# Spread sums, 14 held products, and memory V turned by DMA for the first two head blocks

## The chip, the cores and the metric

The kernel runs on one core of a Trainium2 chip. The metric is device time in microseconds: the median of several runs. One further execution was profiled; its page and trace give the durations used here.

## The reference

Two independent parts, joined along the last axis.

Part A is a linear recurrence over 2048 steps with 1024 complex states:

```
Bu = einsum('bld,pd->blp', x, B_bar)
h  = Lam_bar * h + Bu[:, t]          # for t in 0..2047
y  = 2 * einsum('blp,dp->bld', hseq, Cmat).real + x * Dskip
```

Part B is attention in 64 segments of 32 tokens with 8 memory tokens, 32 heads of 128. Each segment attends to itself (causally) and to the memory, and the output rows of the memory tokens become the next segment's memory:

```
h = concatenate([mem, xs])           # 8 + 32 rows
q, k, v = h @ Wq, h @ Wk, h @ Wv
o = softmax(mask(q k^T * scale)) v;  o = o @ Wo
mem = o[:, :8];  outs.append(o[:, 8:])
```

## The kernel before

The program has four stages, and TensorE has work in all of them.

**Stage 1** (to about 347 us) mixes the first half of part A with the value projection of part B. A list made by `steps()` sets the order: 32 blocks `("s", pc, q)` of part A (8 groups of 128 states, times 4 stretches of 512 time steps; block number n = 4*pc + q) and 32 steps `("v", hb, q)` of the value projection (8 blocks of 4 heads, times 4 stretches of 512 tokens). Most blocks are followed by one value step; after blocks 6, 11, 16, 21, 26 and 30 there is none. `stage1` does 16 matmuls into `psU` (two buffers of two banks). VectorE then multiplies by a table into `a_pr` (L273), adds (L278), and scans (L283, two of them); ScalarE copies the scans to `a_g` (L284); GpSimd works out the carry (L288 to L290). The product with the second table, `a_n` (L297), and its sum, `a_h` (L298), belong to `form()`, which is called inside the next block, between that block's multiply and its add; SP stores `a_h` to `a_hs`. `tables(pc + 1)` is made in block 4*pc + 2. A value step does 32 matmuls into `psP` (three banks), ScalarE copies each bank to a staging buffer `b_vst` (L93; two of these buffers, taken in turn by `next_st`), and ScalarE's queue stores the buffer to `b_vx` in DRAM (L498 to L502).

Between these lies `sum_x`: 16 reductions of `b_xe` (the turned input) to sums over segments (L433), one for each 128 tokens, and a last step that makes `xbar` (L439 to L443). It is a generator, and block n takes two steps of it after `stage1`. `xbar` feeds a guess of the memory rows: `og` multiplies it with the value weights, `guess` with the output weights, and the guess is put into columns of `b_xe` called `memT`.

**Stage 2** (about 347 to 470 us) is the second half of part A: 32 units of 16 matmuls and a VectorE add (`a_ot`, L339); each second unit ScalarE's queue stores `a_ot`. Beside it run the remaining `og`, `guess`, and at the end the memory rows of V for the first two head blocks: `v_mem(0)` and `v_mem(1)`. `v_mem` multiplies weights with `memT`, which gives the rows turned (channels by rows), copies them to `b_vm`, turns them, and stores them to `b_vx` and `b_vt`. For head blocks 2 to 7 (called from stage 3) the turn is a write to DRAM (`b_vmt`) and a DMA transpose into a staging buffer; for 0 and 1 it is four TensorE transposes.

**Stage 3** (about 470 to 1017 us) mixes the q and k projections of a head pair (`proj`) with attention over groups of 96 tokens (`attention`); `load_v` brings values of a head pair from `b_vx` and `b_vt` on SP's queue. **Stage 4** is the output projection. A branch at the end repeats the work step by step should the guess have been too coarse; it isn't taken here.

Instructions are put in order by a planner that works with estimated times and can move an instruction past others of its engine. `keep_in_program_order` holds one at its place in the program. Everything on TensorE is held in stage 1, everything on SP in stages 1 and 2, and on VectorE the 16 reductions, all 32 products L297 and one constant of the check. In stage 3 nothing is held but a few loads. Pools named `p1`, `p2` and so on share memory, and a tile waits until the tile that lay there is done with.

Of the kernel before, what the change touches and what calls it, by code (L numbers as in the profile page):

```python
# [9 lines left out]
BF16 = mybir.dt.bfloat16  # L10
# [24 lines left out]
NMX = 7  # L35
# [9 lines left out]
EO = E + 4  # L45
MW = 4 * GP + 24

XMAIN = 1920
XE = T + NM
XP = 2128  # L50
# [108 lines left out]
class PartA:  # L159
# [101 lines left out]
    def stage1(self, pc, tb):  # L261

        k = self.k; V, S, G, PE = k.V, k.S, k.G, k.PE
        if tb == 0:
            self.carry = None
        self.form, last = None, self.form
        t3, r3 = self.tabs
        u = k.ps("U", (128, 2, TB))
        for i in range(2):
            for c in range(KC):  # L270
                PE.matmul(u[:, i, :], self.bt[:, i, c, :], self.xT[:, c, tb * TB:(tb + 1) * TB], start=(c == 0), stop=(c == KC - 1))
        pr = self.wp.tile([128, 2, 2, TB], FP32, name="a_pr", bufs=2)
        V.tensor_tensor(pr[:], u[:].unsqueeze(1).to_broadcast([128, 2, 2, TB]),  # L273
                        view(t3, [[TB + 1, 2], [TB + 1, 2], [1, TB]]), ALU.mult)
        if last is not None:
            last()
        w = pr[:, :, 0, :]
        V.tensor_tensor(w, w, pr[:, :, 1, :], ALU.add)  # L278
        rb = self.rr[:, pc:pc + 1].to_broadcast([128, TB])
        ini = self.carry  # L280
        g = self.wp.tile([128, 2, TB], BF16, name="a_g", bufs=2)
        for j in range(2):
            V.tensor_tensor_scan(w[:, j, :], rb, w[:, j, :], 0.0 if ini is None else ini[:, j:j + 1], ALU.mult, ALU.add)  # L283
            S.activation(g[:, j, :], w[:, j, :], ACT.Copy)  # L284
        if tb < NB - 1:
            nx = self.wp.tile([128, 2], FP32, name="a_nx", bufs=2); tt = self.wp.tile([128, 2], FP32, name="a_tt", bufs=2)
            for j in range(2):
                G.tensor_scalar(tt[:, j:j + 1], w[:, j, TB - 1:TB], t3[:, 1, TB:TB + 1], None, ALU.mult)  # L288
                G.tensor_scalar(nx[:, j:j + 1], w[:, 1 - j, TB - 1:TB], t3[:, 2 - 2 * j, TB:TB + 1], None, ALU.mult)
            G.tensor_tensor(nx[:], nx[:], tt[:], ALU.add)  # L290
            self.carry = nx

        def form():
            n = self.wp.tile([128, 2, 2, TB], BF16, name="a_n", bufs=1)
            h = self.wp.tile([128, 2, TB], BF16, name="a_h", bufs=2)
            k.tc.keep_in_program_order(
                V.tensor_tensor(n[:], g[:].unsqueeze(1).to_broadcast([128, 2, 2, TB]), view(r3, [[TB, 2], [TB, 2], [1, TB]]), ALU.mult))  # L297
            V.tensor_tensor(h[:], n[:, :, 0, :], n[:, :, 1, :], ALU.add)  # L298
            k.SP.dma_start(self.hs[tb][:, pc, :, :], h[:])
        self.form = form  # L300
# [48 lines left out]
class PartB:  # L349
# [195 lines left out]
        yield  # L545


    def store_t(self, hb, s):

        for r0, n, i in ((0, 2, NMX), (NTL - 3, 2, NMX + 2), (3, NTL - 6, NT4)):  # L550
            self.k.SP.dma_start(self.vt[hb][r0:r0 + n, :].rearrange("n (h e) -> n h e", h=4), s[i:i + n, :, :])

    def v_mem(self, hb, w=None):
        k = self.k
        w = w or self.load_wv(hb)
        p = k.ps("P")
        for h in range(4):
            for c in range(KC):
                k.PE.matmul(p[:, h * NM:(h + 1) * NM], w[:, c, h * 128:(h + 1) * 128], self.memT[:, c, :], start=(c == 0), stop=(c == KC - 1))
        vm = self.vmp.tile([128, 4, 128], BF16, name="b_vm", bufs=1)  # L560
        k.copy("v", vm[:, :, 0:NM], p[:, 0:4 * NM].rearrange("p (h n) -> p h n", h=4))
        if hb > 1:

            k.V.memset(vm[:, :, NM:128], 0.0)
            k.SP.dma_start(self.vmt[hb][:], vm[:].rearrange("p h n -> p (h n)"))
            yield
            s = self.next_st()[:].rearrange("p i h e -> p (i h e)")[:, 0:576].rearrange("p (h e) -> p h e", h=4)
            k.V.memset(s[:, :, E:EW], 1.0)
            k.SP.dma_start_transpose(s[:, :, 0:E], self.vmt[hb][:])
            yield  # L570
            k.SP.dma_start(self.vx[hb][64:64 + NMX, :].rearrange("n (h e) -> n h e", h=4), s[0:NMX, :, 0:EW])
            self.store_t(hb, s[:, :, 0:EW])
            yield
        yield
        pt = k.ps("P", (128, 1024), BF16)
        for h in range(4):
            k.PE.transpose(pt[0:NM, h * 128:(h + 1) * 128], vm[:, h, 0:NM], k.ident[:])
        st = self.next_st()
        k.copy("v", st[0:NM, 0, :, 0:E], pt[0:NM, 0:512].rearrange("p (h e) -> p h e", h=4))
        sv = st[:, 0, :, :].rearrange("p h e -> p (h e)")  # L580
        k.SP.dma_start(self.vx[hb][64:64 + NMX, :], sv[0:NMX, :])
        self.store_t(hb, st[:, 0, :, :])
        yield


# [425 lines left out]
def kernel_main(tc, A_x, A_Lre, A_Lim, A_Bre, A_Bim, A_Cre, A_Cim, A_logdt, A_Dskip, B_x, B_mem0, B_Wq, B_Wk, B_Wv, B_Wo, out,  # L1011
                force=False, dbg=None):
    with ExitStack() as ctx:
# [16 lines left out]
        with pool("p1x", "right") as p1x, pool("p1", "right", 1) as p1:  # L1030
            a.tab = a.tmp = a.wp = a.btp = p1
            k.pin |= {"PE", "SP"}
            warm(k, p1)
            w0 = b.wl.tile([128, KC, 512], BF16, name="b_wv", bufs=2)
            b.load_wv_part(w0, 0, 0, 128, nc.scalar)
            b.x0 = []
            for i in range(2):
                b.load_x0(p1, i)
            b.load_wv_part(w0, 0, 128, 256)
            b.load_wv_part(w0, 0, 256, 512)  # L1040
            b.load_xp(64 + 256, 256, 256)
            wv = {0: w0, 1: b.load_wv(1)}
            consts(k)
            a.load_params(p1)
            b.load_m0(p1)
            b.stage_init()
            order = steps()
            b.v_x(0, 0, wv[0])
            b.load_x(1)
            a.load_b(0)  # L1050
            a.xT = p1x.tile([128, KC, T], BF16, name="a_xT", bufs=1)
            a.load_x(0)
            a.params(p1, p1)
            b.init(p1)
            a.tables(0)
            loads = [[(b, 2)], [(a, 1), (a, 2)], [(b, 3), (a, 3)]]
            sx = b.sum_x(p1)
            tabs = {0: a.tabs}
            bts = {0: a.bt}
            for kind, pc, q in order[1:]:  # L1060
                if loads and kind == "v":
                    for o, n in loads.pop(0):
                        o.load_x(n)
                if kind == "v":
                    b.v_x(pc, q, wv[pc])
                    if q == 3:
                        if pc >= 3:
                            b.og(pc, wv[pc])
                        n = (pc + 2) if pc + 2 < PC else (2, 0)[pc + 2 - PC]
                        wv[n] = b.load_wv(n)  # L1070
                    continue
                a.tabs, a.bt = tabs[pc], bts[pc]
                n = 4 * pc + q
                if q == 2 and pc + 1 < PC:
                    a.load_b(pc + 1)
                    bts[pc + 1], a.bt = a.bt, bts[pc]
                if pc >= 4 and q == 1:
                    a.load_c(pc - 4)
                a.stage1(pc, q)
                for _ in range(2):  # L1080
                    next(sx, None)
                if q == 2 and pc + 1 < PC:
                    a.tables(pc + 1)
                    tabs[pc + 1] = a.tabs
                if n == 12:
                    masks(k)
                    check_consts(k)
                if n == 14:
                    b.fill(p1)
            a.form()  # L1090
            k.pin.remove("PE")
# [7 lines left out]
        with pool("p2h", "right") as p2h, pool("p2", "right") as p2:  # L1099
# [5 lines left out]
            for i, _ in enumerate(s2):  # L1105
                if i in (1, 4, 7):
                    n = (2, 0, 1)[(i - 1) // 3]
                    b.og(n, wv[n], "O")
                    if n == 2:
                        wv[1] = b.load_wv(1)  # L1110
                if i in (3, 7, 11, 15):
                    b.load_wog((3, 7, 11, 15).index(i), p2)
                if i in (9, 11, 13, 15, 17, 19, 21, 22):
                    next(g)
                if i == 20:
                    b.load_wqk(0)
                if i == 23:
                    for _ in g:
                        pass
                if i in (24, 26):  # L1120
                    vm = b.v_mem((i - 24) // 2, wv[(i - 24) // 2])
                if 24 <= i < 28:
                    next(vm)


# [131 lines left out]
```

## Time and profile before

| | us |
|---|---|
| median of 7 runs | 1241.37 (1241.06 to 1241.55) |
| profiled execution | 1241.22 |
| its span, first to last instruction | 1239.5 |
| TensorE busy with matmuls | 1231.1 |
| VectorE, ScalarE, GpSimd busy | 676.2, 266.7, 268.7 |
| granted TensorE clock | 1.00 |

The 1.72 us between the span and the profiled time lie around the span. A row of the timeline gives the start in us, the time in us from the first start to the last end of the instructions merged in it, the engine, the line, the operation, output and input by the program's names, and how many; in brackets at its end stand the idle time of the engine just ahead of it and what ended that. "ACTq" and "SPq" are the engines' DMA issues. In the table of stretches each engine has its busy time in us and its number of instructions, and then come the TensorE clock, the DMA share and GB/s.

### The profile page before, as it was taken

What the parts mean: (1) busy time and instruction counts of PE and PEld (TensorE: products, weight loads), DVE (VectorE), ACT (ScalarE), POOL (GpSimd) and SP (SyncE); (2) the same over time, 40 slices, a digit from 0 to 9 for tenths busy, and PEclk for the clock granted to TensorE, in tenths of its full rate; (3) what the DMA queues carried; (4) which work ended last, traced back from release to release, by engine and by line L of the source; (5) the groups of instructions that cost most, each with busy time, mean ns of one, the idle gap of its engine ahead of it and who ended that gap; (6) DMA issues with size and microseconds to landing.
All of it is one profiled execution on the core that took longest, in us unless ns stands there. A gap on an engine that the chain in (4) does not pass through costs nothing.

```text
span 1239.5 us, 20045 instructions
## 1 busy us (share of the span) xinstructions
PE 1231.1 (99%) x8174; PEld 654.8 (53%) x8174; DVE 676.2 (55%) x1270; ACT 266.7 (22%) x694; POOL 268.7 (22%) x437
## 2 busy tenths in 40 slices
PE   9999999999999999999999999999999999999998
PEld 4444444444445555656565656555565554445444
DVE  4799999988721124666666666656666641001000
ACT  5344444443310000112121111212111210000000
POOL 4111221212222321222222222223222320000000
PEclk9999999999999999999999999999999999999999
DMA  9942455563798834765464645536474279407000
GB/s 242 249 148 79 139 139 131 158 157 98 212 319 257 268 111 103 211 145 129 108 153 108 153 108 117 137 89 138 113 148 103 58 208 248 102 18 154 18 17 27
DMA packets 321268, 174.20 MB, mean 141 GB/s; under 512 B 145882, under 2 KB 308876, under 8 KB 321172
## 3 DMA queue, kind: packets, MB, share of 16 engines
q1 hardware_dynamic: 299076, 145.33, 48.8%
q10 hardware_dynamic: 21072, 24.38, 5.9%
q0 software_dynamic: 1024, 3.17, 0.7%
q8 instruction: 65, 1.06, 0.4%
q14 instruction: 31, 0.25, 0.1%
HBM read 84.42 MB, written 53.96 MB: 112 GB/s over the span
## 4 chain that ended last, share of the span: by engine, by line
PE 92%; DVE 4%; DMA 2%; issue 1%; SPq 1%; ACT 0%; ACTq 0%; DVEq 0%
PE psP L68 78%; PE psU L68 7%; PE psS L68 3%; PE psO L68 2%; PE psR L68 1%; DMA b_vx<-b_vst 1%; DVE a_pr L283 1%; DVE a_pr L273 1%; DVE b_xr L433 1%; SPq L68 1%; DVE a_pr L278 1%; DMA b_wv<-in_B_Wv_dram 0%; ACT b_vst L93 0%; DVE a_h L298 0%; DVE a_tabh L239 0%
## 5 line engine op out<-in xcount | busy, mean ns | idle before, releaser
L68 PE MATMUL psP<-b_xe,b_wk 128*128 128x480 bf16 (+1 forms) x1280 | 247.5, 343 | 0.0
L68 PE MATMUL psP<-b_xe,b_wq 128*128 128x480 bf16 (+1 forms) x1280 | 247.5, 343 | 0.0
L68 PE MATMUL psP<-b_wv,b_xe 128*128 128x512 bf16 (+2 forms) x1048 | 224.8, 373 | 2.5 <-ACT b_vst L93 2.1
L685 POOL TENSOR_TENSOR b_m<-b_e,maskB 99x396 bf16<-99x396 bf16 (+1 forms) x160 | 134.4, 840 | 335.9 <-ACT b_e L684 335.9
L684 ACT ACTIVATE b_e<-psS 99x396 bf16<-99x396 f32 (+3 forms) x208 | 91.3, 441 | 530.7 <-PE psS L68 522.3
L68 PEld LDWEIGHTS <-b_wk 128*128 128x128 bf16 x1280 | 119.2, 98 | 94.2
L68 PEld LDWEIGHTS <-b_xe 128*128 128x128 bf16 x1056 | 101.8, 98 | 122.1 <-issue 3.4
L68 PEld LDWEIGHTS <-b_wq 128*128 128x128 bf16 x1280 | 118.5, 98 | 87.8
L95 DVE CAST b_k<-psP 128x480 bf16<-128x480 f32 (+1 forms) x192 | 97.3, 528 | 100.4 <-PE psP L68 100.4
L95 DVE CAST b_q<-psP 128x480 bf16<-128x480 f32 (+1 forms) x192 | 97.3, 528 | 92.2 <-PE psP L68 90.9
L68 PEld LDWEIGHTS <-b_ol 128*128 128x128 bf16 x864 | 84.3, 98 | 94.4
L68 PE MATMUL psU<-a_xT,a_bt 128*128 128x512 bf16 x512 | 114.8, 379 | 0.0
L68 PE MATMUL psP<-t,a_hl 128*128 128x512 bf16 x512 | 113.1, 379 | 0.0
L95 DVE CAST b_ost<-psP 128x512 bf16<-128x512 f32 (+1 forms) x17 | 11.5, 676 | 177.6 <-PE psP L68 177.6
L93 ACT ACTIVATE b_vst<-psP 128x512 bf16<-128x512 f32 x126 | 72.8, 590 | 108.5 <-PE psP L68 101.2
L68 PE MATMUL psP<-wo,b_ol 128*128 128x512 bf16 (+1 forms) x448 | 92.5, 364 | 0.0
L68 PE MATMUL psP<-t,b_ol 128*128 128x512 bf16 x416 | 92.2, 379 | 0.0
L288 POOL TENSOR_SCALAR a_tt<-a_pr,a_tabf 128x1 f32<-128x1 f32 x48 | 36.6, 762 | 251.3 <-DVE a_pr L283 251.3
L702 DVE TENSOR_TENSOR b_ob<-psO,b_accR 99x384 bf16<-99x384 f32 x160 | 86.0, 554 | 2.6 <-DVE b_accR L701 0.4
L273 DVE TENSOR_TENSOR a_pr<-psU,a_tabf 128x2048 f32<-128x2048 f32 x32 | 73.0, 2282 | 26.4 <-PE psU L68 26.4
L68 PEld LDWEIGHTS <-a_bt 128*128 128x128 bf16 x512 | 49.8, 98 | 59.5
L68 PEld LDWEIGHTS <-a_hl 128*128 128x128 bf16 x512 | 49.1, 98 | 56.7
(203 smaller groups left out, 963.5 us busy)
## 6 DMA issues: line engine op xcount, KB each, us to landing
b_v<-b_vx SPq DMA_DIRECT2D x16, 1122.0 KB
b_wv<-in_B_Wv_dram SPq DMA_DIRECT2D x16, 1024.0 KB
b_vx<-b_vst ACTq DMA_DIRECT2D x24, 544.0 KB
b_on<-b_ob SPq DMA_DIRECT2D x15, 720.0 KB
a_hs<-a_h SPq DMA_DIRECT2D x32, 256.0 KB
b_wog<-in_B_Wo_dram SPq DMA_DIRECT2D x4, 2048.0 KB
b_wq<-in_B_Wq_dram SPq DMA_DIRECT2D x16, 512.0 KB
b_wk<-in_B_Wk_dram SPq DMA_DIRECT2D x16, 512.0 KB
```

The lines of the kernel that those rows point to most:

```text
L68: r = f(*a, **kw)
L93: self.S.activation(out, in_, ACT.Copy)
L95: self.V.tensor_copy(out, in_)
L273: V.tensor_tensor(pr[:], u[:].unsqueeze(1).to_broadcast([128, 2, 2, TB]), view(t3, [[TB + 1, 2], [TB + 1, 2], [1, TB]]), ALU.mult)
L278: V.tensor_tensor(w, w, pr[:, :, 1, :], ALU.add)
L283: V.tensor_tensor_scan(w[:, j, :], rb, w[:, j, :], 0.0 if ini is None else ini[:, j:j + 1], ALU.mult, ALU.add)
L288: G.tensor_scalar(tt[:, j:j + 1], w[:, j, TB - 1:TB], t3[:, 1, TB:TB + 1], None, ALU.mult)
L433: r = V.tensor_reduce(xs[:, :, 4 * j:4 * j + 4], self.xe[:, :, 128 * j:128 * j + 128].rearrange("p c (s t) -> p c s t", s=4), AX.X, ALU.add)
L684: k.S.activation(e[:, a:b, :, 0:n], s[0:GW, a:b, :, 0:n], ACT.Exp, scale=float(E) ** -0.5, accum_out=self.accE[0:GW, j:j + 1])
L685: k.G.tensor_tensor(mv[:, a:b, :, 0:n], e[:, a:b, :, 0:n], mask[0:GW, :, 0:n].unsqueeze(2).to_broadcast([GW, b - a, 2, n]), ALU.mult)
L702: V.tensor_tensor(self.ob[:, b0:b0 + n, :], o[0:GW, 0:n, 0:E], r.unsqueeze(2).to_broadcast([GW, n, E]), ALU.mult)
```

## The change

1. Block 0 takes two steps of `sum_x` ahead of `stage1` and three after it; blocks 1 to 9 take 2, 2, 2, 0, 2, 1, 1, 1, 1. It was two after each block until the 17 steps were through.
2. The product L297 is held in program order for the first 14 blocks (`HELD`) alone.
3. `v_mem` turns by DMA for every head block. For the first two, all its DMAs (the write, the transpose and the four stores) are issued on ScalarE's queue; the calls take three units of stage 2 each, from units 24 and 27, in place of two from 24 and 26.

```diff
+HELD = 14
...
+        held = NB * pc + tb < HELD
+
         def form():
...
-            k.tc.keep_in_program_order(
-                V.tensor_tensor(n[:], g[:].unsqueeze(1).to_broadcast([128, 2, 2, TB]), view(r3, [[TB, 2], [TB, 2], [1, TB]]), ALU.mult))
+            i = V.tensor_tensor(n[:], g[:].unsqueeze(1).to_broadcast([128, 2, 2, TB]), view(r3, [[TB, 2], [TB, 2], [1, TB]]), ALU.mult)
+            if held:
+                k.tc.keep_in_program_order(i)
...
-    def store_t(self, hb, s):
+    def store_t(self, hb, s, q):
...
-            self.k.SP.dma_start(self.vt[hb][r0:r0 + n, :].rearrange("n (h e) -> n h e", h=4), s[i:i + n, :, :])
+            q.dma_start(self.vt[hb][r0:r0 + n, :].rearrange("n (h e) -> n h e", h=4), s[i:i + n, :, :])
...
         k.copy("v", vm[:, :, 0:NM], p[:, 0:4 * NM].rearrange("p (h n) -> p h n", h=4))
-        if hb > 1:
...
+        q = k.SP if hb > 1 else k.nc.scalar
+        k.V.memset(vm[:, :, NM:128], 0.0)
+        q.dma_start(self.vmt[hb][:], vm[:].rearrange("p h n -> p (h n)"))
         yield
-        pt = k.ps("P", (128, 1024), BF16)
-        for h in range(4):
-            k.PE.transpose(pt[0:NM, h * 128:(h + 1) * 128], vm[:, h, 0:NM], k.ident[:])
-        st = self.next_st()
-        k.copy("v", st[0:NM, 0, :, 0:E], pt[0:NM, 0:512].rearrange("p (h e) -> p h e", h=4))
...
+        s = self.next_st()[:].rearrange("p i h e -> p (i h e)")[:, 0:576].rearrange("p (h e) -> p h e", h=4)
+        k.V.memset(s[:, :, E:EW], 1.0)
+        q.dma_start_transpose(s[:, :, 0:E], self.vmt[hb][:])
+        yield
+        q.dma_start(self.vx[hb][64:64 + NMX, :].rearrange("n (h e) -> n h e", h=4), s[0:NMX, :, 0:EW])
+        self.store_t(hb, s[:, :, 0:EW], q)
         yield
...
+                for _ in range(2 if n == 0 else 0):
+                    next(sx)
                 a.stage1(pc, q)
-                for _ in range(2):
-                    next(sx, None)
+                for _ in range((3, 2, 2, 2, 0, 2, 1, 1, 1, 1)[n] if n < 10 else 0):
+                    next(sx)
...
-                if i in (24, 26):
-                    vm = b.v_mem((i - 24) // 2, wv[(i - 24) // 2])
-                if 24 <= i < 28:
+                if i in (24, 27):
+                    vm = b.v_mem((i - 24) // 3, wv[(i - 24) // 3])
+                if 24 <= i < 30:
                     next(vm)
```

More of the change, by code (lines that the diff above doesn't have):

```diff
@@ L561, in v_mem @@
         k.copy("v", vm[:, :, 0:NM], p[:, 0:4 * NM].rearrange("p (h n) -> p h n", h=4))
-        if hb > 1:
[L564 to L573, printed above, removed]
-        yield
-        pt = k.ps("P", (128, 1024), BF16)
-        for h in range(4):
-            k.PE.transpose(pt[0:NM, h * 128:(h + 1) * 128], vm[:, h, 0:NM], k.ident[:])
-        st = self.next_st()
-        k.copy("v", st[0:NM, 0, :, 0:E], pt[0:NM, 0:512].rearrange("p (h e) -> p h e", h=4))
-        sv = st[:, 0, :, :].rearrange("p h e -> p (h e)")
-        k.SP.dma_start(self.vx[hb][64:64 + NMX, :], sv[0:NMX, :])
-        self.store_t(hb, st[:, 0, :, :])
+        q = k.SP if hb > 1 else k.nc.scalar
+        k.V.memset(vm[:, :, NM:128], 0.0)
+        q.dma_start(self.vmt[hb][:], vm[:].rearrange("p h n -> p (h n)"))
+        yield
+        s = self.next_st()[:].rearrange("p i h e -> p (i h e)")[:, 0:576].rearrange("p (h e) -> p h e", h=4)
[4 more added lines that the diff above has]
+        self.store_t(hb, s[:, :, 0:EW], q)
         yield
```

## The prediction

> **What bounds the kernel now.** I read the page first: TensorE carries the span, and the chain that ended last is almost all TensorE.
>
> ```profile
> PE 1231.1 (99%) x8174; PEld 654.8 (53%) x8174; DVE 676.2 (55%) x1270; ACT 266.7 (22%) x694; POOL 268.7 (22%) x437
> PE 92%; DVE 4%; DMA 2%; issue 1%; SPq 1%; ACT 0%; ACTq 0%; DVEq 0%
> ```
>
> Busy time alone does not say that TensorE runs at its peak, so I took the spacing of matmul starts from the trace. A 512-column matmul follows the one before by 0.216 us nearly everywhere. After the start-up, 10 us in, gaps worth more than 0.1 us above that spacing are few: 1.10 us at 120.1, 0.43 at 131.6, 0.81 at 336.0, 0.45 at 343.7, and about 0.1 at 1152.6. The first four sum to 2.79 us. **This is all that better ordering can give back**; everything else on TensorE is work.
>
> The second view is the busy time by stretch (columns: PE, PEld, DVE, ACT, POOL, clock, DMA):
>
> ```profile
> 40.00:60.00 20.00, 20.00 (x94) 9.11 (x93) 17.51 (x15) 7.48 (x13) 4.09 (x10) 1.00 1.11 252
> 100.00:120.00 20.00, 20.00 (x94) 9.11 (x93) 20.00 (x17) 7.48 (x14) 4.03 (x10) 1.00 0.36 111
> 120.00:140.00 20.00, 18.80 (x88) 8.32 (x86) 19.95 (x23) 8.38 (x16) 5.32 (x7) 1.00 0.41 121
> 180.00:200.00 20.00, 20.00 (x94) 9.08 (x93) 14.79 (x13) 8.52 (x15) 2.07 (x5) 1.00 0.43 127
> 320.00:340.00 20.00, 19.35 (x90) 8.71 (x89) 14.95 (x12) 6.80 (x12) 6.47 (x13) 1.00 0.52 181
> ```
>
> VectorE has 2.5 us free at 40 to 60, nothing from 100 to about 180, then slack again. TensorE loses matmuls (88 and 90 for 94) where VectorE is full, and at the end of the stage.
>
> The third view, the timeline, shows how the loss happens:
>
> ```profile
> 117.77 2.45 DVE L283 TENSOR_TENSOR_SCAN a_pr<-a_rr,a_nx,a_pr 128x512 f32<-128x512 f32 x2
> 120.25 0.63 ACT L284 ACTIVATE a_g<-a_pr 128x512 bf16<-128x512 f32 x1
> 120.79 0.58 ACT L93 ACTIVATE b_vst<-psP 128x512 bf16<-128x512 f32 x1
> 121.42 1.89 PE L68 MATMUL psP<-b_wv,b_xe 128*128 128x512 bf16 x8 [0.94 <-ACT b_vst L93]
> ...
> 337.04 7.07 PE L68 MATMUL psP<-b_wv,b_xe 128*128 128x512 bf16 x32 [0.65 <-ACT b_vst L93]
> ...
> 343.75 1.57 ACT L93 ACTIVATE b_vst<-psP 128x512 bf16<-128x512 f32 x3 [4.19 <-DMA b_vx<-b_vst]
> 344.40 1.89 PE L68 MATMUL psP<-b_wv,b_xe 128*128 128x512 bf16 x8 [0.29 <-ACT b_vst L93]
> ```
>
> The scan of block 7 ends late on VectorE; ScalarE stands in front of its copy of that scan (`a_g`); the copies out of `psP` queue behind it; the three `psP` banks are full; TensorE stops. At 343.75 the cause is another: ScalarE waits for a staging buffer whose store, issued at 331.87, lands 11.8 us later.
>
> [...] the trace agrees (a 512-column matmul has 0.379 us of duration but 0.216 us of spacing), so I count spacing. [...]
>
> **The change, part by part.** Blocks are numbered n = 4*pc + q, 0 to 31.
>
> *Sums earlier.* Still 17 steps. Finished after blocks 0 to 9: 5, 7, 9, 11, 11, 13, 14, 15, 16, 17; before: 2, 4, 6, 8, 10, 12, 14, 16, 17, 17. One sum is 1.16 us of VectorE (two take 2.32). Two now stand before block 0, when VectorE is free (6.4 us idle before 33.70), and their columns of `b_xe` are turned by TensorE before 10 us. The third extra one falls into the 2 us gap between the sums at 45.21 and the multiply of block 1 near 49.7. So 3 x 1.16 = 3.5 us moves into idle time. It is taken out after block 4 (two) and block 6 (one). A VectorE block with two sums takes 9.68 us (multiplies at 112.70 and 122.38), so 8.5 with one.
>
> Working it forward: the multiply of block 5, today at 93.35, comes at 91.0, when its matmuls are done. That of block 6, today 103.03, would be at 100.7, but its matmuls end near 101.4: 0.7 us idle. Block 7: 101.4 + 8.5 = 109.9 for today's 112.70, so the scan ends 7.5 later, at 117.4 for 120.2, and ScalarE's copy frees the bank at about 118.6. TensorE wants it at 120.3. **Gap of 1.10 gone, cover 1.7 us.** Block 8: multiply 118.4, scan ends 125.9, with the table step and the copies the bank is free near 128.3; TensorE, 1.1 us earlier than today, wants it at 130.7. **Gap of 0.43 gone, cover 2.4 us.** After that VectorE is about 2.8 us earlier and TensorE 1.53, so no new gap. `xbar`, today at 130, comes a block later; its first reader is the `og` product at 168.46. The sums cost nothing else. Sum: -1.53.
>
> *Products held in 14 blocks.* No instruction goes or comes; 18 products (1.22 us each, with a 0.69 add behind) may move. There is slack on VectorE there, and TensorE loses nothing between 132 and 336. The likely new place is the wait for matmuls, such as the 2.83 us before 320.89, ahead of the next multiply. At the end this brings the scan of block 31 about 1.9 us forward, enough for the 0.81 gap; but the next one hangs on the store that lands at 343.66, and TensorE would only arrive there earlier and wait longer. The product of block 31 (347.59, today behind the `og` copy) can start near 336.5, but its store stays behind a weight load on SP's queue, at 349.56. Bounds for the part: nothing, or -1.26 if the store is early as well; a loss is possible where a product gets ahead of a multiply that is ready (1.9 us, against about 2.7 us of cover at a bank, 255.73 to 258.4). I take -0.2.
>
> *Memory V turned by DMA.* Removed: eight TensorE transposes, 0.055 us apart, 0.22 us for each head block (448.15 to 448.37 and 456.32 to 456.54), with no wait around them: **-0.44**. Also removed: two VectorE copies of 0.41 and eight SP issues; added: four memsets (0.25 and 0.09) on VectorE, which has 2.5 us idle per unit of 3.45; and on ScalarE's queue per head block one write, one transpose and four stores. That chain is seen on SP for head block 2: write issued 567.23, transpose 569.22, last store issued by 577.7, so 10.5 us. On ScalarE's queue it starts near 445.7 and 456.9 (the second matmuls now start a unit later, at 455.0) and ends near 456 and 468. Behind it wait only three output stores with two buffers; the first Exp is at 486.42, a cover of 18 us. `load_v(0)` needs the first chain, landed near 458; today its long load is issued at 460.70, takes SP 16.2 us, and is first used at 491.43. SP is freed of the second set of stores, the weight load for `v_mem(3)` moves 3 us. Cost 0 under those covers; without them it is what the chain overruns.
>
> **Sum:** 1.53 + 0.2 + 0.44 = 2.17 us off the profiled execution (1241.22: span 1239.5 and 1.72 around it): 1239.05. The median of the runs is 0.15 higher, so **1239.2**. A change under 0.2% (2.48 us) can't be told from none by this measurement.
>
> **Rivals.**
>
> 1. *All gaps go* (0.15): 2.79 + 0.44 = 3.23 off, 1238.1. For it: the 0.81 gap is a VectorE lateness that the freed products should cure. Against: the DMA at 343.66.
>
> 2. *The sums only move the lateness*, or the planner does not place them early: VectorE is full until 180 and the totals by block 7 are alike. Then only the transposes and the tail count: -0.5, 1240.9. Against: 3.5 us of real idle time before.
>
> 3. *Slower: VectorE waits for the new DMA chain.* The planner pulls the memsets of head blocks 2 and 3 (L568 at 452.73 and 460.98) directly behind the stores that free their staging buffer. Now these stores end the 10.5 us chain, about 458 and 470. If VectorE stands at such a memset while `psP` fills, TensorE stops. In stage 2 there is cover of two units (6.9 us), in the first projections of two groups of 1.62 us. A memset that waits 6 us in the projections costs 6 - 3.2 = 2.8, twice that with the `b_vm` memset; net +0.6 to +3.4, 1242 to 1244.8. It decides from a wait of 3.2 us there plus the 2.2 gained. For it: VectorE already waited for DMA semaphores before 452.73. Against: the order is planned with DMA times in mind.
>
> 4. *The transpose on ScalarE's queue isn't what runs*: then the ident matmuls remain and 0.44 is missing; unlikely (0.03), it is written out.
>
> **How the numbers follow.** Main case 0.55, 1238.6 to 1239.8; its better quarter (0.13) passes the bound. All gaps 0.15, rival 2 with 4 0.10, slower 0.20 (with planner moves in the attention that I can't see). So faster 0.13 + 0.15 = 0.28, same 0.42 + 0.10 = 0.52, slower 0.20. Range: from 1237.6 (all gaps and run scatter) to 1244.0, which takes in most of rival 3.
>
> **What would show it.** Right: 94 matmuls in each 20 us from 100 to 200; no PE wait near 120; five sums before 50 us; no `psP<-ident,b_vm` group; transposes of `b_vst` on ACTq for two head blocks; first att_back matmul about 2 us earlier. Wrong: a PE wait ended by a DVE instruction between 450 and 490; new PE gaps between 180 and 330; a first Exp later than 486.

## The result, and the profile after

| | before | after |
|---|---|---|
| median, us | 1241.38 (34 runs) | 1244.65 (14 runs, 1244.24 to 1246.4) |
| ratio, with its 95% interval | | 1.0028 [1.0021, 1.0035] |
| profiled execution, and its span | 1241.22, 1239.5 | 1245.2, 1243.4 |

The change makes the kernel **slower by 3.3 us**. The forecast was 1239.2 with a range up to 1244.0, so the kernel moved the other way, to just outside the range.

The page still shows a TensorE that is busy for 99% of the span, with eight matmuls fewer (the transposes). In the chain that ended last VectorE's share has gone from 4% to 0, and the DMA's from 2% to 3%:

```profile
PE 1232.0 (99%) x8166; PEld 654.5 (53%) x8166; DVE 679.9 (55%) x1272; ACT 266.4 (21%) x694; POOL 271.6 (22%) x437
PE 96%; DMA 3%; SPq 1%; ACTq 0%; DVE 0%; issue 0%; DVEq 0%
```

In the table of stretches (PE, PEld, DVE, ACT, POOL, clock, DMA share, GB/s) stage 1 has its matmuls back: 95, 94 and 95, where 94, 88 and 90 stood. The loss is at the end of stage 2, with 2.98 us of PE missing from 440 to 460, and 2.20 from 460 to 480 at a granted clock of 0.91. The first row is the kernel before, where nothing was missing there:

```profile
440.00:460.00 20.00, 20.00 (x155) 10.48 (x154) 5.31 (x11) 0.00 (x0) 6.90 (x5) 1.00 0.53 167
```

```profile
100.00:120.00 20.00, 20.00 (x95) 9.01 (x94) 19.41 (x16) 8.04 (x15) 2.12 (x5) 1.00 0.27 91
120.00:140.00 20.00, 20.00 (x94) 9.08 (x93) 19.96 (x23) 7.77 (x15) 4.56 (x10) 1.00 0.47 134
320.00:340.00 20.00, 20.00 (x95) 9.00 (x94) 14.78 (x12) 6.74 (x12) 7.09 (x14) 1.00 0.60 214
440.00:460.00 20.00, 17.02 (x134) 8.71 (x132) 3.04 (x7) 0.00 (x0) 2.78 (x2) 1.00 0.43 136
460.00:480.00 20.00, 17.80 (x95) 9.28 (x95) 6.21 (x26) 0.00 (x0) 4.14 (x6) 0.91 0.22 69
```

By the spacing of matmul starts, all four gaps of stage 1 are gone (2.79 us). New, counted above the usual spacing, are a stop of 3.48 us at 456.64, eight matmuls after it at up to 0.427 us instead of 0.216 (1.5 us more), and a stop of 2.02 us at 473.51, where the matmuls have 199 columns and a spacing of 0.086: **7.0 us**. So 7.0 - 2.79 - 0.44 = 3.8 us longer; the span grew by 3.9 and the median by 3.3.

The timeline of the queues, VectorE and TensorE points to the cause. The first row merges two loads of weights, issued at 442.20 and 453.60. The rows of ACTq are head block 0's *chain*: the write, the transpose, which needs the write's data, and the four stores, which need the transpose's. A DMA *lands* when its data have arrived.

```profile
442.20 11.78 SPq L69 DMA_DIRECT2D b_wv<-in_B_Wv_dram  x2
...
442.70 0.34 ACTq L568 DMA_DIRECT2D b_vmt<-b_vm  x1
448.06 1.32 ACTq L572 DMA_TRANSPOSE b_vst<-b_vmt  x1
...
450.79 1.41 ACTq L574 DMA_DIRECT2D b_vx<-b_vst  x1
...
452.24 2.33 ACTq L555 DMA_DIRECT2D b_vt<-b_vst  x3
...
459.60 0.09 DVE L571 MEMSET b_vst<- 128x32 bf16 x1 [9.73 <-DMA b_vt<-b_vst]
459.60 0.68 DVE L343 TENSOR_TENSOR a_ot<-psP,a_xd 128x512 bf16<-128x512 f32 x1
...
460.34 12.05 PE L69 MATMUL psP<-t,a_hl 128*128 128x512 bf16 x48 [3.31 <-DVE a_ot L343]
...
474.78 0.09 DVE L571 MEMSET b_vst<- 128x32 bf16 x1 [8.52 <-DMA b_vt<-b_vst]
...
475.62 1.53 PE L69 MATMUL psP<-b_xe,b_wk 128*128 128x199 bf16 x16 [1.86 <-DVE a_ot L343]
```

The 0.09 us memset of ones at 459.60 prepares a staging buffer for head block 2. In the kernel before the same memset waited for nothing:

```profile
452.73 0.09 DVE L568 MEMSET b_vst<- 128x32 bf16 x1
```

Here it stands in VectorE's queue ahead of the add that empties `psP`, and it waits 9.73 us until the last store of head block 0's chain has left that buffer, 16.7 us after the chain's write was issued (442.70; the store landed at 459.44). Meanwhile `psP` fills and TensorE stops. It happens again at 474.78, for head block 3 behind head block 1.

The view of waits (total, times, longest), here from 440 to 480, puts both kinds of memset side by side; the second kind is the zeros of `b_vm`:

```profile
DVE b_vst L571 <- DMA b_vt<-b_vst: 18.3, 2, 9.7
...
DVE b_vm L567 <- DMA b_vmt<-b_vm: 9.8, 2, 5.5
...
PE psP L69 <- DVE a_ot L343: 5.2, 2, 3.3
```

### The profile page after: what moved, and what is told of

It reads as the page before. It is cut to its first block, busy times and chain, and to the rows that moved or that the text cites. A ratio compares the mean times of both kernels' runs of the same rounds, so it can differ in the third digit from the quotient of the medians.

```text
span 1243.4 us, 20035 instructions
## 1 busy us (share of the span) xinstructions
PE 1232.0 (99%) x8166; PEld 654.5 (53%) x8166; DVE 679.9 (55%) x1272; ACT 266.4 (21%) x694; POOL 271.6 (22%) x437
## 3 DMA queue, kind: packets, MB, share of 16 engines
q0 software_dynamic: 1024, 3.17, 0.7%
## 4 chain that ended last, share of the span: by engine, by line
PE 96%; DMA 3%; SPq 1%; ACTq 0%; DVE 0%; issue 0%; DVEq 0%
PE psP L69 80%; PE psU L69 9%; PE psS L69 3%; PE psO L69 2%; PE psR L69 1%; DMA b_vt<-b_vst 1%; DMA b_vmt<-b_vm 1%; SPq L69 1%; DMA b_wv<-in_B_Wv_dram 0%; DMA b_vst<-b_vmt 0%; ACTq L555 0%; ACTq L574 0%; DVE a_ot L343 0%; DVE b_vm L96 0%; DVE b_ost L96 0%
```

## Experiments

I asked three questions: does each part bring what it was priced at; does the memset make the stop; and why is the chain 16.7 us long? Each kernel's edit is against the changed kernel, except for the four under "The parts alone", which apply one or two parts to the kernel before. All times are medians, with the ratio to the kernel before on the same chip.

### The parts alone

**Sums earlier, alone**

```diff
+                for _ in range(2 if n == 0 else 0):
+                    next(sx)
                 a.stage1(pc, q)
-                for _ in range(2):
-                    next(sx, None)
+                for _ in range((3, 2, 2, 2, 0, 2, 1, 1, 1, 1)[n] if n < 10 else 0):
+                    next(sx)
```

> The kernel before with the early sums alone. The prediction's step: both TensorE gaps near 120 and 131 us (1.10 and 0.43) go, so 1.5 us less than before, about 1239.8. If the products also had to be let loose for that, one of the two gaps stays and the gain is 1.1 or less. The gaps at 336 and 344 (0.81 and 0.45) should stay.

Measured: 1239.74, ratio 0.9988 [0.9981, 0.9994], which is -1.56 us with an interval of -2.4 to -0.7, so a change below the 2.48 us that the prediction took for the limit does show here. Both gaps near 120 and 131 are gone. At the end of the stage the gap of 0.81 stays, and the other grows from 0.45 to 0.94: TensorE gets there earlier and waits longer for the same store. By its gaps this kernel gains 1.53 - 0.49 = 1.04, inside the interval.

**14 products held, alone**

```diff
+        held = NB * pc + tb < HELD
...
+            if held:
+                k.tc.keep_in_program_order(i)
```

> The kernel before with the products held in the first 14 blocks only. The gaps near 120 and 131 stay. If the late scan of block 31 is all that causes the end of the stage to stall, the gap of 0.81 goes, and the one of 0.45 behind the store grows by as much (net 0, as the prediction had it); if the store comes early as well, both go: 1.26 us less, about 1240.1.

Measured: 1240.04, ratio 0.9989 [0.9983, 0.9996], -1.26 us. Both gaps at the end of stage 1 are gone, the other two stay, and a small one of about 0.18 us appears at 201.7, in the stretch where the prediction wanted to see no new ones (the changed kernel has none there). The timeline shows the product moved, as the prediction had it, into the wait for the matmuls. But the wait for the store, expected to stay, has more than halved (4.19 us at 343.75 before):

```profile
317.48 1.23 DVE L296 TENSOR_TENSOR a_n<-a_g,a_tabh 128x2048 bf16<-128x2048 bf16 x1 [0.70 <-ACT a_g L284]
...
321.03 2.29 DVE L273 TENSOR_TENSOR a_pr<-psU,a_tabf 128x2048 f32<-128x2048 f32 x1 [1.59 <-PE psU L68]
...
340.82 0.60 ACT L93 ACTIVATE b_vst<-psP 128x512 bf16<-128x512 f32 x1 [1.94 <-DMA b_vx<-b_vst]
```

The store was issued later than before (334.60 for 331.87) and landed earlier (340.8 for 343.7). Before, it was issued between GpSimd's four `a_hl` loads (330.02 to 332.24); here it comes 3.6 us after them. The trace's DMA records fit this: before, the store's 512 packets ran for 6.5 us with 429 packets of GpSimd's loads among them; here they run for 2.3 us with 80 among them. No run moved the store alone.

**The DMA turn, alone**

```diff
-        if hb > 1:
+        q = k.SP if hb > 1 else k.nc.scalar
...
+        k.V.memset(s[:, :, E:EW], 1.0)
+        q.dma_start_transpose(s[:, :, 0:E], self.vmt[hb][:])
...
-                if i in (24, 26):
+                if i in (24, 27):
```

> The kernel before with the DMA turn of memory V on ScalarE's queue alone. If the loss of the changed kernel sits wholly in the waits of VectorE's memsets on that chain: 0.44 us less for the transposes and 6.9 us more for the gaps seen near 457, 461 and 474, so about 6.4 us more than before, 1247.8. If the loss needs the new order of stage 1 (TensorE arriving earlier), clearly less than that, 4 us or under.

Measured: 1247.15, ratio 1.0048 [1.0034, 1.0062], +5.85 us. The stop (3.5 us at 459.2), slow matmuls after it (the next three units took 12.21 us, where 0.216 us a matmul makes 10.5) and a second stop (1.5 at 476.3) are all there. The loss belongs to this part alone.

**Sums and 14 held, without the DMA turn**

> The kernel before with the early sums and the products held in 14 blocks, memory V turned on TensorE as before. If the two parts work on different gaps, their gains (1.56 and 1.26) add: 2.8 less than before, about 1238.5, and no gap above 0.1 us between 100 and 480 us. If they share VectorE's slack, one of them is worth less: 1239 or more.

Measured: 1238.45, ratio 0.9977 [0.9967, 0.9986], -2.95 us, as much as the two alone (1.56 + 1.26 = 2.82) and as the four gaps (2.79). The parts add up.

### Is it the memset?

**Fills made once.** The fills are the two kinds of memset. The zeros go into two fixed `b_vm` buffers at the start of the program; the ones are written only in the first round of the two staging buffers.

```diff
+        self.vms = [c.tile([128, 4, 128], BF16, name=f"b_vm{i}") for i in range(2)]
...
+        for vm in self.vms:
+            k.G.memset(vm[:, :, NM:128], 0.0)
...
-        vm = self.vmp.tile([128, 4, 128], BF16, name="b_vm", bufs=1)
+        vm = self.vms[hb % 2]
-        k.V.memset(vm[:, :, NM:128], 0.0)
...
-        k.V.memset(s[:, :, E:EW], 1.0)
+        if hb < 2:
+            k.V.memset(s[:, :, E:EW], 1.0)
```

> The changed kernel, but the zeros of b_vm are written once, at the start, into two fixed buffers, and the ones of the staging buffers only for head blocks 0 and 1 (the later head blocks find them in place). So no memset in stages 2 and 3 has to wait for the DMA chain; the chain itself is unchanged. Memset theory: the gaps of 6.9 us go, 3.2 us less than before, about 1238.2. If the chain's length on ScalarE's queue (late V, late output stores) or the planner's order in the attention is what costs, the time stays above 1241.

Measured: 1242.53, ratio 1.0007 [1.0001, 1.0014], 4.3 us above the expectation. The stops at 457 and 474 are gone, so the memset theory holds for them. But **a second wall**, another wait that stops TensorE, stood behind the first: TensorE now waits in the attention for the values of V. The first row below is the load of V in the kernel before, the others are this kernel's (the row of a load merges a small first part and the main one).

```profile
460.43 16.49 SPq L68 DMA_DIRECT2D b_v<-b_vx  x2
```

```profile
464.20 16.99 SPq L69 DMA_DIRECT2D b_v<-b_vx  x2
...
491.23 0.50 PE L69 MATMUL psO<-b_v,b_m 128*128 128x129 bf16 x6 [2.96 <-DMA b_v<-b_vx]
```

The main load of V came 9 us later than before (issued at 469.62 instead of 460.70), and landed at 491.19. In the changed kernel it came later still (472.91, landed 494.15) and cost nothing, because TensorE, some 7 us later by its stops, asked for it only at 495.32. The one loss hid the other. The profiled execution, at 1240.87, is among this kernel's shortest; its runs reach from 1240.3 to 1243.8, which the last section takes up.

**Only the ones written once**, and **only the zeros written once**, split that edit.

> The changed kernel with only the ones of the staging buffers written once; the zeros of b_vm are still written each time. If the memsets of the staging buffers make the two gaps (waits of 9.7 and 8.5 us, beyond the cover), the gaps near 457 and 474 go and the wait for V of e4_once is left: 1240.5 to 1243. If the b_vm memsets (waits of 5.5 and 4.2) are enough for a gap: 1244 or more.

> The other half: the zeros of b_vm once, the ones of the staging buffers each time. If the staging memsets make the gaps: 1243 to 1245, with gaps of some 2 us or more near 457 and 474. If both kinds are needed for a gap: as e4_once, 1240.5 to 1243.

Measured: ones once, 1242.89, 1.0009 [1.0000, 1.0017]; zeros once, 1244.96, 1.0036 [1.0022, 1.0049]. With the ones written once, VectorE still waits up to 7.8 us at a memset of zeros and TensorE doesn't stop near 457; with the zeros written once, it stops as before. These are the waits of VectorE, first in the kernel with the ones once, then in the one with the zeros once:

```profile
DVE b_vm L567 <- DMA b_vmt<-b_vm: 13.3, 2, 7.8
```

```profile
DVE b_vst L573 <- DMA b_vt<-b_vst: 17.0, 2, 9.8
```

**The memset of ones makes the stop.** A wait of 7.8 us at the zeros was covered, one of 9.8 at the ones was not.

### Why is the chain so long?

**The chain on SP's queue**

```diff
-        q = k.SP if hb > 1 else k.nc.scalar
+        q = k.SP
```

> The changed kernel with the DMA chain of the first two head blocks on SP's queue in place of ScalarE's. Theory that VectorE's memsets wait for the chain, whatever queue it is on: the gaps near 457 and 474 stay, 1243 to 1247. Theory that ScalarE's queue is what is slow: the chain takes about 10.5 us as for head block 2, the gaps go, 1239.5 or less.

Measured: 1246.0, ratio 1.0040 [1.0026, 1.0054]. This fits neither expectation. The first hop, from the issue of the write to that of the transpose, is just as long (442.55 to 448.08), so leaving ScalarE's queue doesn't shorten it; but here the write comes behind a load of weights on its own queue. The stops at 457 and 474 are gone: the second load of weights is now issued at 454.18, behind the chain's stores, the last of them lands at 456.89 instead of 459.44, and the memsets of ones wait only 3.1 and 4.5 us. Yet the time is no better. The load of V now stands behind both chains on SP (main load 468.18, landed 494.24), and the wait at it, with slow matmuls after it (480 columns at 0.400 us for 0.202), is the loss.

```profile
PE psO L69 <- DMA b_v<-b_vx: 5.9, 1, 5.9
```

**Weight loads held back.** In the changed kernel SP issues the two loads of value weights for head blocks 2 and 3 (1 MB each) at 442.20 and 453.60. The first goes out 0.5 us ahead of the write of head block 0's chain, the second 0.1 us ahead of that chain's last store (453.67, landed 459.44). Here they come in stage 3 and are held there; nothing else in the program differs.

```diff
+    def load_wv_late(self, hb):
+        w = self.wl.tile([128, KC, 512], BF16, name="b_wv", bufs=2)
+        self.k.tc.keep_in_program_order(self.k.SP.dma_start(w[:], self.Wf[2][:, :, hb * 512:hb * 512 + 512]))
+        return w
...
+            if hp == 0 and u in (5, 8):
+                late[2 + u // 8] = b.load_wv_late(2 + u // 8)
...
-                    vm = b.v_mem(hp // 2 + 1)
+                    vm = b.v_mem(hp // 2 + 1, late.pop(hp // 2 + 1, None))
```

> The changed kernel, but the two 1 MB weight loads for head blocks 2 and 3, which SP issues at 442.2 and 453.6 as the chain starts, are held back to stage 3. Theory that the chain's hops are long (5.4 us for the write, 5.8 for the last store) because these loads share the DMA engines: hops of 2 to 3 us, VectorE waits about 4 us less at each memset, the gaps of 6.9 us fall to 1.5 or less: 1238 to 1240. Theory that the hops are long by themselves: no change, 1244.6.

Measured: **1237.79**, ratio 0.9972 [0.9961, 0.9983], -3.6 us: faster than both kernels. The memsets are still there and still wait, but only 2.75 us for the first and 5.98 for the second, and TensorE has no wait left from 440 to 520:

```profile
442.41 0.34 ACTq L573 DMA_DIRECT2D b_vmt<-b_vm  x1
444.14 1.32 ACTq L577 DMA_TRANSPOSE b_vst<-b_vmt  x1
...
448.16 2.33 ACTq L560 DMA_DIRECT2D b_vt<-b_vst  x3
...
452.33 0.09 DVE L576 MEMSET b_vst<- 128x32 bf16 x1 [2.75 <-DMA b_vt<-b_vst]
...
459.78 16.93 SPq L69 DMA_DIRECT2D b_v<-b_vx  x2
...
466.91 0.09 DVE L576 MEMSET b_vst<- 128x32 bf16 x1 [5.98 <-DMA b_vt<-b_vst]
```

The first hop takes 1.7 us (442.41 to 444.14) instead of 5.4, the last store 2.5 to its landing instead of 5.8, and the chain 9.7 (to 452.1) instead of 16.7. From 440 to 450 the DMA engines were busy for 0.18 of the time here, and 0.42 in the changed kernel (next to the last column); these are the two rows, this kernel's first:

```profile
440.00:450.00 10.00, 10.00 (x75) 5.12 (x74) 2.78 (x5) 0.00 (x0) 2.50 (x2) 1.00 0.18 55
```

```profile
440.00:450.00 10.00, 10.00 (x76) 5.04 (x74) 2.63 (x5) 0.00 (x0) 1.53 (x2) 1.00 0.42 131
```

The trace's DMA records show the write's packets behind the load's. Issued at 442.70, its 128 packets start from 446.25 on, when 766 of the load's 1024, the first of them at 443.23, have started; without the load they start at 443.26. The store of stage 1 above had 429 packets of GpSimd's loads among its own; here most of the load has started before the write's first packet. Why, no run tested. What the runs show is that the hop of this write, issued 0.5 us behind a 1 MB load of another queue, is longer by 3.7 us than without that load. The main load of V moved up as well, to 464.98; it landed at 486.62 and was used at 488.02. **With the weight loads held back neither wall stands.** Early, they lengthen the chains (head block 0's to 16.7 us from 9.7), for which VectorE's memsets wait and behind which the load of V comes. The DMA turn is then worth about its price: 1237.79 with it and 1238.45 without it, 0.66 us for the 0.44 forecast, with intervals that overlap.

**Both edits together** (fills once, weight loads held back):

> Both cures: the fills written once (as in e4_once) and the weight loads held back (as in e7_late). In e4_once TensorE then waited 3 us at 488 us for V. If that wait comes from the same long hops (the load of V is behind the chain of head block 1), it goes: 3.2 us less than before, 1238.1 with little scatter. If V is late for another reason, 1240 to 1243 as in e4_once.

Measured: 1237.74, ratio 0.9971 [0.9959, 0.9982]. Nothing is gained over the late weight loads alone: here the memsets, whose wait is covered, cost nothing (1237.79 with them).

### What holds the load of V?

In the changed kernel's waits of SP's queue, from 440 to 512, two lines belong to the two loads of head pair 0:

```profile
SPq L69 <- DMA b_vst<-b_vmt: 7.6, 1, 7.6
...
SPq L69 <- DMA b_vx<-b_vst: 5.2, 1, 5.2
```

These loads read head block 0, but here they wait for the transpose and a store of head block **1**. By the changed kernel's trace it is no dependence of data. The transpose and the first load carry one semaphore, number 118: the transpose landed at 467.47, and the load, which waits for 118, went out at 467.49. The store and the main load carry number 100: landed 472.89, issued 472.91. To test whether head block 1's chain holds the load, that chain was moved into stage 3, on SP's queue (with the fills once, and the weight loads early as in the changed kernel).

```diff
-        q = k.SP if hb > 1 else k.nc.scalar
+        q = k.SP if hb > 0 else k.nc.scalar
+        if hb == 1:
+            yield
...
-                if 24 <= i < 30:
+                if 24 <= i < 28:
...
+            if hp == 0 and u in (4, 6, 8):
+                next(vm)
```

> As e4_once (fills written once, weight loads early), but the DMA chain of head block 1 is issued in stage 3 on SP's queue, behind the first loads of V. In e4_once the two loads of V (reading head block 0) went out at the moment at which transfers of head block 1's chain landed. Theory that V is late only because its loads stand behind that chain: they go out near 460 or before, no wait of TensorE at 488, 1238 to 1238.8. If the load of V is late through the weight loads themselves, the wait stays: 1240 to 1243.

Measured: 1246.47, ratio 1.0039 [1.0025, 1.0053]; missed. The run didn't do what its edit meant: the planner took the chain back ahead of the load (454.17 to 467.8), whose main part was issued at 468.66 and landed at 494.29. TensorE waited for it, and the granted clock of the profiled execution was 0.997 on average, where the kernel before has 1.00.

```profile
PE psO L69 <- DMA b_v<-b_vx: 5.8, 1, 5.8
```

The same, with the six DMAs of that chain held in program order:

```diff
+        def kp(i):
+            if hb == 1:
+                k.tc.keep_in_program_order(i)
```

> e9_once_chain1 again, with the transfers of head block 1's chain held in program order on SP, so that they really come behind the first loads of V (in e9_once_chain1 the planner moved them ahead, and the loads of V went out at 468.3). The weight loads stay early. Theory that V is late because its loads stand behind the chain of head block 1: they go out near 460, V lands before 488, no wait of TensorE there: 1237.7 to 1238.8. If V is late through the weight loads alone, the wait at 488 stays, 1240 to 1243.

Measured: 1237.72, ratio 0.9971 [0.9960, 0.9983], where the fills once alone gave 1242.53. SP's timeline has the load ahead of the chain again, and no wait of TensorE is left, though the weight loads are as early as in the changed kernel:

```profile
441.95 11.78 SPq L69 DMA_DIRECT2D b_wv<-in_B_Wv_dram  x2
...
460.82 0.27 SPq L69 DMA_DIRECT2D b_v<-b_vt  x1
461.14 16.72 SPq L69 DMA_DIRECT2D b_v<-b_vx  x2
```

So, with the weight loads early, the second wall is the place of the V load behind head block 1's chain. That the shared semaphore alone holds it, in the kernels with the chain on ScalarE's queue, is read from the trace; no run changed the semaphores by themselves.

## Why the prediction failed

**What bounds the kernel: right.** The four gaps were worth 2.79 us, and all four went.

**Sums earlier, -1.53: right, with one omission.** Alone, the part gave 0.49 of its gaps back at the store of stage 1, which "so no new gap" had left out. The worked path shows in the changed kernel's timeline, with the multiplies of blocks 6, 7 and 8 at 101.61, 110.17 and 118.72, where 101.4, 109.9 and 118.4 were forecast, and the scan of block 7 over at 117.7 (117.4):

```profile
101.61 2.29 DVE L274 TENSOR_TENSOR a_pr<-psU,a_tabf 128x2048 f32<-128x2048 f32 x1 [0.59 <-PE psU L69]
...
110.17 2.28 DVE L274 TENSOR_TENSOR a_pr<-psU,a_tabf 128x2048 f32<-128x2048 f32 x1
...
115.24 2.46 DVE L284 TENSOR_TENSOR_SCAN a_pr<-a_rr,a_nx,a_pr 128x512 f32<-128x512 f32 x2
```

**14 held, -0.2: the term was too small**, and measured -1.26, the far bound. The failing step was "the next one hangs on the store that lands at 343.66": the landing was taken as fixed. It moved by 2.9 us when the issues around it moved.

**DMA turn, -0.44 and "Cost 0 under those covers": here the sign went wrong.** The transposes went, as priced. The cost was 7.0 us in place of 0, by three steps of the working. The third made the stops; the first made them longer; the second hid the next one.

1. The chain's length, 10.5 us, came from head block 2's row, and it ends with the issue of the last store, which landed at 579.31: 12.1 us after the write's issue, for 16.7 here. That row is no quiet moment (from 565 to 580 the DMA engines were busy for 0.71 of the time, with a 1 MB load at 571.72), but no 1 MB load of another queue was issued just ahead of its steps. The write's hop took 2.0 us there and 5.4 here. Of the loads of weights in this stretch the prediction says only that one "moves 3 us".

```profile
567.23 0.54 SPq L68 DMA_DIRECT2D b_vmt<-b_vm  x1
569.22 1.91 SPq L68 DMA_TRANSPOSE b_vst<-b_vmt  x1
571.72 0.38 SPq L68 DMA_DIRECT2D b_wv<-in_B_Wv_dram  x1
```

2. The cover of the V load was counted from today's issue (460.70) to today's first use (491.43). The load landed at 486.75, some 10 us after SP had done issuing it, so the real cover was 4.7 us. The change moved the load by 12.
3. The working asked who waits behind ScalarE's queue and found only covered work, and it priced the memsets by their 0.25 and 0.09 us. The one that waited was VectorE, for a buffer that the chain reads: its memset of ones waited 9.73 us. The length of the chain is not the whole of it. The chain started 3 us sooner than forecast and landed at 459.44, where the forecast had "near 458"; had it landed at 458, TensorE would still have stopped for about 2 us, an estimate from the 3.48 us less the 1.44.

**The rival "VectorE waits for the new DMA chain" is what happened**, given 0.20. It named the instruction, the head blocks and both memsets; its top price, 1244.8, is close to 1244.65. Its mechanism is right, but that nearness is partly luck. The first stop comes in stage 2, where the rival counted two units of cover (6.9 us): the wait of 9.73 ran over. And its price had no half-rate matmuls. The words against it, "the order is planned with DMA times in mind", were no evidence: the planned order had the wait of 9.73 us in it. The sign that was to show the forecast wrong, a TensorE wait ended by VectorE between 450 and 490, is in the profile twice.

**What stays open.** The gaps account for 3.23 us of the 3.6 that the late weight loads gain over the kernel before; the other 0.4 was not placed. Why the store of stage 1 lands earlier is read from the trace and not tested. Why the write's packets start so late behind a load of the other queue isn't known.

## What to carry to other kernels

A price for a chain of small dependent DMAs must come from a moment with the same neighbours: ask which large loads the new order puts just ahead of its steps, on any queue (here the write's hop took 5.4 us behind a load of SP's, and 1.7 without it). When a DMA is put in place of compute, list which instructions wait for its buffers and what stands behind them, above all fills ahead of an instruction that empties PSUM (here the memset of ones, 9.73 us), and which later loads come behind it. A cover ends where the data land, not where the issue ends (486.75, not 476.9, for the load of V in the kernel before); and when one wall falls, look for the next wait before counting the gain.

## What the runs showed of the hardware

**A stop can cost more than its own length.** After the stop of 3.48 us, TensorE ran at half rate for 2.9 us (0.427 us a matmul for 0.216), and after the 6.1 us of the chain on SP's queue at 0.400 for 0.202 (480 columns; three of them took 1.41 us, and 0.77 with the fills once). After 2.02 us it ran at full rate (0.085 us a matmul of 199 columns, for 0.086 ahead of the stop). With the DMA turn alone, the three units after the stop of 3.53 us took 12.21 us, 1.7 more than 0.216 a matmul makes. Stops of 3.1 us go both ways: no slow matmul followed with the fills once (the wait of 2.96 us shown above), and nearly 6 us of half rate with the ones once (a wait of 2.94). This is the latter's row of stretches, with a clock of 0.66, and its first eight 480-column matmuls after the stop, which took 1.78 us in the other:

```profile
490.00:500.00 10.00, 8.89 (x45) 4.70 (x45) 3.60 (x9) 0.63 (x3) 0.87 (x1) 0.66 0.17 46
```

```profile
491.71 3.41 PE L69 MATMUL psP<-b_xe,b_wk 128*128 128x480 bf16 x8
```

So a stop of 3.1 us was followed by half rate in one of two profiled runs; what decides it, no run showed. The runs of those two kernels scatter over some 3.5 us (1240.3 to 1243.8 with the fills once). That this difference is the reason is my estimate, from these two profiles, and was not shown.
